# Top-32 attention and mixture of depths on one core: each stage of a unit in a step of its own

## The chip, the core and the metric

The kernel runs on one core of one Trainium2 chip. The core has TensorE (PE in the profile, with PEld for its weight loads), VectorE (DVE), ScalarE (ACT), GpSimd (POOL) and SyncE (SP, which here only issues DMAs); each works through its own queue in order. The metric is the device time of one execution in microseconds (us), the median of the runs shown. A lower time is better.

## The reference

The input has 8 batches, 8 heads, 576 tokens and 64 numbers per head and token. For every query the 32 largest of its 576 scores are kept, the rest is masked out, and the softmax of what is left weighs the values. The heads of a token are then put side by side (512 numbers), and in each batch the 128 tokens with the largest gate score pass through a two-layer network; its result, times a sigmoid of the gate, is added to them.

```python
scores = scale * np.matmul(q, k.transpose(0, 1, 3, 2))
kth = np.partition(scores, -top_k, axis=-1)[..., -top_k:-top_k + 1]
scores = np.where(scores >= kth, scores, -1000000000.0)
attn = np.exp(scores - np.max(scores, axis=-1, keepdims=True))
attn = attn / (np.sum(attn, axis=-1, keepdims=True) + 1e-09)
x = np.matmul(attn, v)                       # then (B, S, H*D)
scores = np.einsum('bsd,d->bs', x, w_gate)
top_idx = np.argpartition(-scores[b], capacity)[:capacity]
h = np.maximum(x[b, top_idx] @ w1, 0.0)
out[b, top_idx] = x[b, top_idx] + g[:, None] * (h @ w2)
```

All of it is computed in 32-bit floats. A second version of the whole computation stands behind a branch at the end (`general`); it runs only if a check on the device says that the fast way was not safe, and it does not run on these inputs.

## The kernel before, in words

**Units.** A unit is a batch, a query tile t and a pair of heads (line 513): 8 x 5 x 4 = 160 units. The 576 queries are cut into four tiles of 128 and a last one of 64 (`J = 4`, `JP = 512`, `R = 64`). A unit with t below 4 has two tiles of 128 queries, one per head (a whole unit); for t = 4 the 64 queries of both heads lie one above the other in one tile (a half unit, `heads_of`, line 219). Keys are split in the same way, 4 x 128 and 64.

**What a unit goes through.** (1) `multiply` (227): scores on PE into a PSUM tile `ps`; `keep` (242): ACT copies them to `sc`. (2) `bound` (252): DVE takes the 8 largest of each of 8 pieces (`cand`) and merges these 64 candidates in three rounds (`best`), which gives a lower bound for the 32nd score; POOL puts it into `seen` (the cast at line 270). (3) `part` (275): ACT forms the sign of score minus bound (`sides`); `mask` (290): POOL multiplies scores by it and adds 8 counters (`y`). (4) `find_kth` (302): DVE's maximum of `y` (`next8`), POOL scales it into `seen` (307). (5) Lines 544 to 556: ACT forms a steep ramp below the 32nd score (`z`, Relu), POOL subtracts it from the scores (`z`), so that what is masked out lies very low. (6) `turn` (309): PE transposes `z`, four blocks of 128 keys into `ptr` and the last 64 keys into `small`; ACT takes the exponential of both into `pT` (581, 589). (7) `values` (317): PE multiplies `pT` with the values `v`, for each head four blocks of 128 keys and one of 64, into `small`; ACT copies the result to `xs` (331).

**The loop.** One loop over n (line 530) runs all stages of different units side by side. Step n issues, in this order: loading of later inputs in the first steps (533), `multiply` of unit n+1 (536), the ramp and subtraction of unit n-2 (544), `keep` of n+1 (557), `values` of n-3 (559), `bound` of n (567), then tile by tile `part` and `mask` of n beside `turn` and exponential of n-2 (574), `find_kth` of n-1 (596), the gate of a finished token tile (600), one piece of the mixture (607), `normalise` (608) and a piece of loading the next batch (614). So `bound`, `part` and `mask` of one unit stand in one step, and so do the ramp, the transposes and the exponentials of another. `InOrder` (33) keeps PE, DVE, ACT and POOL in exactly the order in which the program issues; all instructions that pass through it have line 41 in the profile. DMAs are issued by SP in program order.

**The mixture.** `mixture` (388) is a generator that a batch's end starts; each step of the next batch takes one piece of it: the gate row (`route`, 348), ranks of the tokens (two DVE passes per tile with the table `before`, 370 to 386), one-hot picks, the gathered tokens (`xe_ps`, 40 PE instructions), two parts of the first layer (`h_ps`, 32 each), the second layer (`y_ps`, 16 of 512 columns) and an indirect DMA that adds the result to the output (481).

**Buffers.** PSUM: `ps` two tiles of two banks, `ptr` two banks, and two banks that `small`, the transposes of the loads (`tr`) and all of the mixture share (lines 84 to 86). SBUF: `sc` four buffers, `z`, `y`, `sides`, `cand`, `pT` two each.

Of the kernel before, what the change touches and what calls it, by code (L numbers as in the profile page):

```python
# [44 lines left out]
def kernel(  # L45
# [38 lines left out]
    ps_sc = ctx.enter_context(tc.tile_pool(name="ps_sc", bufs=2, space=PS))  # L84
    ps_tr = ctx.enter_context(tc.tile_pool(name="ps_tr", bufs=2, space=PS))
    ps_small = ctx.enter_context(tc.tile_pool(name="ps_small", bufs=2, space=PS))
# [28 lines left out]


    before = const.tile([P, NT, S], BF16, name="before")
    nc.gpsimd.memset(before[:, 0:J, JP:S], 0.0)
    nc.gpsimd.memset(before[:, 0:J, 0:JP], 1.0)
    nc.gpsimd.memset(before[:, J, :], 1.0)  # L120
    for t in range(J):
        nc.gpsimd.affine_select(
            out=before[:, t, 0:JP].rearrange("p (j i) -> p j i", j=J),
            in_=before[:, t, 0:JP].rearrange("p (j i) -> p j i", j=J),
            compare_op=ALU.is_gt,
            fill=0.0,
            base=t,
            pattern=[[-1, J], [-J, P]],
            channel_multiplier=J,
        )  # L130
    nc.gpsimd.affine_select(
        out=before[:, J, JP:S],
        in_=before[:, J, JP:S],
        compare_op=ALU.is_gt,
        fill=0.0,
        base=0,
        pattern=[[-1, R]],
        channel_multiplier=1,
    )
# [3 lines left out]
    for i in range(2):  # L143
        vt = const.tile([P, H, NT, DE], FP32, name=f"v{i}")
        nc.gpsimd.memset(vt, 1.0)
        vbufs.append(vt)
# [17 lines left out]
    def room_for_qkv(b):  # L164

        qT = kqpool.tile([P, NHP, S], FP32, name="qT")
        kT = kqpool.tile([P, NHP, S], FP32, name="kT")
        return qT, kT, vbufs[b % 2]

    def load_qkv(qb, kb, vb, qT, kT, vt):  # L170


        def fetch(src, hp, name):
            rows = ldpool.tile([P, NT, 2, D], FP32, name=name, tag="rows")
            for hh in range(2):
                nc.sync.dma_start(
                    out=rows[:, 0:J, hh, :],
                    in_=src[2 * hp + hh, 0:JP, :].rearrange("(p j) d -> p j d", j=J),
                )
            nc.sync.dma_start(  # L180
                out=rows[0:R, J, :, :],
                in_=src[2 * hp : 2 * hp + 2, JP:S, :].rearrange("h p d -> p h d"),
            )
            return rows

        todo = [
            (src, dst, hp, name)
            for hp in range(NHP)
            for src, dst, name in ((kb, kT, "kin"), (qb, qT, "qin"))
        ]  # L190
        fetched = {}
        for i, (src, dst, hp, name) in enumerate(todo):
            for j in range(i, min(i + 3, len(todo))):
                if j not in fetched:
                    fetched[j] = fetch(todo[j][0], todo[j][2], todo[j][3])
            rows = fetched[i]
            tr = ps_small.tile([P, 512], FP32, name="tr", tag="small")
            for c in range(J):
                pe.transpose(
                    tr[:, c * P : (c + 1) * P],  # L200
                    rows[:, c, :, :].rearrange("p h d -> p (h d)"),
                    ident,
                )
            act.copy(out=dst[:, hp, 0:JP], in_=tr)
            tr = ps_small.tile([P, 512], FP32, name="tr", tag="small")
            pe.transpose(
                tr[:, 0:R],
                rows[0:R, J, :, :].rearrange("p h d -> p (h d)"),
                ident[0:R, 0:R],
            )  # L210
            act.copy(out=dst[:, hp, JP:S], in_=tr[:, 0:R])
            nc.sync.dma_start(
                out=vt[:, i, 0:J, 0:D],
                in_=vb[i, 0:JP, :].rearrange("(p j) d -> p j d", j=J),
            )
            nc.sync.dma_start(out=vt[0:R, i, J, 0:D], in_=vb[i, JP:S, :])
            yield
# [9 lines left out]
    def multiply(t, hp, qT, kT):  # L227

        n = R if t == J else P
        pss = [ps_sc.tile([P, 2, 512], FP32, name="ps") for _ in heads_of(t)]  # L230
        for half in range(2):
            for ps, heads in zip(pss, heads_of(t)):
                for hh, r in heads:
                    d = slice(hh * D, (hh + 1) * D)
                    pe.matmul(
                        ps[r : r + n, half, 0:HALF],
                        qT[d, hp, t * P : t * P + n],
                        kT[d, hp, half * HALF : (half + 1) * HALF],
                    )
        return pss  # L240

    def keep(pss):

        sc = scpool.tile([P, 2, S], FP32, name="sc")
        for i, ps in enumerate(pss):
            act.copy(
                out=sc[:, i, :].rearrange("p (u s) -> p u s", u=2),
                in_=ps[:, :, 0:HALF],
            )
        return sc  # L250

    def bound(n, sc, at):

# [7 lines left out]
        for i in range(n):  # L261
            for u in range(8):
                dve.max(cand[:, i, 8 * u : 8 * u + 8], sc[:, i, u * w : (u + 1) * w])
            for r in range(3):
                dve.max(best[r][:, i, :], cand[:, i, :])
                if r < 2:
                    dve.match_replace(
                        cand[:, i, :], best[r][:, i, :], cand[:, i, :], LOWEST
                    )
        pool.tensor_copy(  # L270
            out=seen[:, 0, at : at + n],
            in_=best[2].rearrange("p i e -> p (i e)").bitcast(BF16)[:, 15 : 16 * n : 16],
# [29 lines left out]
    def find_kth(n, y, at):  # L302

        next8 = stats.tile([P, 2, 8], FP32, name="next8")
        for i in range(n):
            dve.max(next8[:, i, :], y[:, i, :])
        pool.tensor_scalar_mul(seen[:, 1, at : at + n], next8[:, 0:n, 7], BIG)

    def turn(i, z, tr, small):

        for c in range(J):
            pe.transpose(
                tr[:, c * P : (c + 1) * P], z[:, i, c * P : (c + 1) * P], ident
            )
        pe.transpose(small[0:R, i * P : (i + 1) * P], z[:, i, JP:S], ident)

    def values(t, hp, pT, small, vt, xs):

        n = R if t == J else P
        for i, heads in enumerate(heads_of(t)):  # L320
            for hh, r in heads:
                for c in range(NT):
                    rows = R if c == J else P
                    pe.matmul(
                        small[0:n, 2 * P + hh * DE : 2 * P + (hh + 1) * DE],
                        pT[0:rows, c, i, r : r + n],
                        vt[0:rows, 2 * hp + hh, c, :],
                        start=(c == 0),
                        stop=(c == J),
                    )  # L330
        act.copy(
            out=xs[0:n, 2 * hp : 2 * hp + 2, :].rearrange("p h e -> p (h e)"),
            in_=small[0:n, 2 * P : 2 * P + 2 * DE],
# [14 lines left out]
    def route(gate, rank):  # L348

        gate_row = modpool.tile([P, S], FP32, name="gate_row")  # L350
        tr = ps_small.tile([P, 512], FP32, name="tr", tag="small")
# [7 lines left out]
        tr = ps_small.tile([P, 512], FP32, name="tr", tag="small")  # L359
# [5 lines left out]
        for t in range(NT):  # L365
            if t == 3:
                yield
            n = R if t == J else P
            tied = modpool.tile([P, S], FP32, name="tied", tag="scratch")
            dve.scalar_tensor_tensor(  # L370
                out=tied[0:n, :],
                in0=gate_row[0:n, :],
                scalar=gate[0:n, t : t + 1],
                in1=before[0:n, t, :],
                op0=ALU.is_equal,
                op1=ALU.mult,
            )
            dve.scalar_tensor_tensor(
                out=tied[0:n, :],
                in0=gate_row[0:n, :],  # L380
                scalar=gate[0:n, t : t + 1],
                in1=tied[0:n, :],
# [3 lines left out]
            )  # L386

    def mixture(row0, x, gate):
# [4 lines left out]
        rank = modpool.tile([P, NT], FP32, name="rank")  # L393
        yield from route(gate, rank)
# [30 lines left out]
        ps = ps_small.tile([P, 512], FP32, name="xe_ps", tag="small")  # L425
# [14 lines left out]
        ps = ps_small.tile([P, 512], FP32, name="extra_ps", tag="small")  # L440
# [10 lines left out]
        dve.tensor_copy(out=row_i, in_=ps[:, 0:1])  # L451
# [4 lines left out]
        for f0 in range(0, NFC, 4):  # L456
            yield
            ps = ps_small.tile([P, 512], FP32, name="h_ps", tag="small")
# [14 lines left out]
        ps = ps_small.tile([P, 512], FP32, name="y_ps", tag="small")  # L473
# [41 lines left out]
    load_from = per_batch - 1 - 2 * NHP  # L515
# [5 lines left out]
    loading = load_qkv(q[0], k[0], v[0], *qkv[0])  # L521
    mixing = iter(())
    gating = None
    xs = x = gate = None
    scs, masked, turned = {}, {}, {}

    def tiles_of(n):
        return len(heads_of(units[n][1]))

    for n in range(-1, len(units) + 4):  # L530
        is_unit = lambda i: 0 <= i < len(units)

# [3 lines left out]
        pss = None  # L536
        if is_unit(n + 1):
            b, t, hp = units[n + 1]
            pss = multiply(t, hp, *qkv[b][0:2])
# [4 lines left out]
        if is_unit(n - 2):  # L544
# [12 lines left out]
        if pss is not None:  # L557
            scs[n + 1] = keep(pss)
        if is_unit(n - 3):
            b, t, hp = units[n - 3]  # L560
# [5 lines left out]
            values(t, hp, *turned.pop(n - 3), qkv[b][2], xs)  # L566
        if is_unit(n):
# [192 lines left out]
```

## Time and profile before

| What | Before |
|---|---|
| Median of 3 runs (lowest to highest) | 1587.45 us (1572.88 to 1592.38) |
| The profiled execution, its own time | 1579.77 us |
| Its span, first to last instruction | 1578.0 us |
| Mean granted PE clock, as a share of full speed | 0.756 |
| Busy: PE, DVE, POOL, ACT | 1345.1, 1077.1, 1003.9, 887.5 us |
| First score copies of batches 1 to 7 | 185.4, 376.7, 568.0, 759.3, 950.7, 1141.2, 1332.5 us |
| Last exponential of the last unit; end | 1526.4; 1578.0 us |

How to read it: a row of the timeline gives the start, the time until the last of its instructions ended, the engine, the operation, what it writes and reads, and how many instructions were merged; in brackets the idle time of the engine before it and what ended it. PE and PEld rows of one matmul belong together: PEld loads the stationary side, PE moves the other through the array. A 32-bit matmul stands as two instructions, a transpose as one. "PEclk" is the share of its full clock that PE was granted.

From one score copy of a whole unit to the next the steps of the later batches take 8.4 to 14.3 us, and the pattern repeats from batch to batch, every 191.3 us or so.

### The profile page before, as it was taken

To read this page: it belongs to the slowest core of one execution; us is meant where nothing else is said; L and a number is where in the kernel's file an instruction comes from. 1 tells how busy PE (TensorE), PEld (TensorE's weight loads), DVE (VectorE), ACT (ScalarE), POOL (GpSimd) and SP (SyncE) were. 2 spreads that over 40 slices of the span, in tenths; PEclk is the share of its full clock that TensorE was granted. 3 is DMA by queue.
4 is the path that set the end of the run, shared out by engine and by line. 5 is a ranking of instruction groups with operands and counts; after the bars stand their busy time and mean duration, and the time that the engine had idled before them with its cause. 6 is when DMAs were issued, how large, how long until landed. Compare 5 with 4: busy or idle time off the path is not lost.

```text
span 1578.0 us, 24253 instructions
## 1 busy us (share of the span) xinstructions
PE 1345.1 (85%) x7322; PEld 1047.6 (66%) x7322; DVE 1077.1 (68%) x5024; ACT 887.5 (56%) x1953; POOL 1003.9 (64%) x1253
## 2 busy tenths in 40 slices
PE   5988888888889879988789887998888988889866
PEld 3766667676677657767568665786666766677554
DVE  4786598656986469764797549875499654987631
ACT  3666565655555555555655556565565665555630
POOL 4776676665766657665666657666576665766730
PEclk9677867967679685786868768597766977679767
DMA  7301200012001120011200112001120011000000
GB/s 177 80 1 31 72 19 1 16 31 73 11 2 22 31 72 5 1 23 31 73 4 1 30 31 69 1 1 31 46 53 1 1 37 35 4 1 7 1 31 9
DMA packets 120507, 45.95 MB, mean 29 GB/s; under 512 B 116144, under 2 KB 116144, under 8 KB 119344
## 3 DMA queue, kind: packets, MB, share of 16 engines
q1 hardware_dynamic: 119216, 42.23, 10.8%
q0 software_dynamic: 1152, 2.10, 1.0%
q8 instruction: 60, 0.98, 0.3%
q14 instruction: 79, 0.65, 0.1%
HBM read 32.77 MB, written 11.53 MB: 28 GB/s over the span
## 4 chain that ended last, share of the span: by engine, by line
PE 42%; DVE 29%; POOL 12%; ACT 10%; issue 6%; DMA 0%; SPq 0%; POOLq 0%; ACTq 0%
PE small L41 18%; DVE cand L41 13%; PE ps L41 7%; POOL z L41 6%; PE ptr L41 6%; DVE best L41 5%; DVE tied L41 5%; ACT sides L41 4%; PE h_ps L41 3%; PE xe_ps L41 3%; DVE next L41 3%; PE y_ps L41 3%; ACT pT L41 3%; PE tr L41 3%; POOL y L41 2%
## 5 line engine op out<-in xcount | busy, mean ns | idle before, releaser
L41 PEld LDWEIGHTS small<-v,pT 128*128 128x128 f32 (+3 forms) x3200 | 492.3, 230 | 150.2 <-ACT pT L41 55.0
L41 PE MATMUL small<-v,pT 128*128 128x65 f32 (+3 forms) x3200 | 560.0, 329 | 16.3 <-ACT pT L41 15.7
L41 POOL TENSOR_TENSOR y<-sc,sides 128x576 f32<-128x576 f32 x288 | 375.3, 1303 | 271.1 <-ACT sides L41 242.0
L41 POOL TENSOR_TENSOR z<-sc,z 128x576 f32<-128x576 f32 x288 | 410.7, 1446 | 153.3 <-ACT z L41 152.3
L41 DVE MAX8 cand<-sc 128x8 f32<-128x72 f32 x2304 | 333.6, 217 | 124.5 <-ACT sc L41 124.5
L41 PE MATMUL ptr<-ident,z 128*128 128x128 f32 x1152 | 251.2, 358 | 101.7 <-POOL z L41 100.9
L41 ACT ACTIVATE z<-sc,seen 128x576 f32<-128x576 f32 x288 | 208.9, 768 | 153.0 <-POOL seen L41 152.9
L41 DVE MAX8 next<-y 128x8 f32<-128x584 f32 x288 | 210.2, 755 | 104.6 <-POOL y L41 104.2
L41 ACT ACTIVATE sides<-sc,seen 128x576 bf16<-128x576 f32 x288 | 222.0, 771 | 104.7 <-POOL seen L41 104.3
L41 PE MATMUL ps<-kT,qT 64*128 64x288 f32 (+1 forms) x1280 | 273.4, 549 | 1.5 <-ACT qT L41 1.5
L41 PEld LDWEIGHTS ptr<-ident,z 128*128 128x128 f32 x1152 | 171.2, 180 | 143.8 <-POOL z L41 133.6
L41 DVE MAX8 best<-cand 128x8 f32<-128x64 f32 x864 | 197.0, 228 | 29.8
L41 PEld LDWEIGHTS ps<-kT,qT 64*128 64x128 f32 (+1 forms) x1280 | 144.8, 230 | 53.1 <-issue 19.9
L41 ACT COPY sc<-ps 128x576 f32<-128x576 f32 x288 | 168.7, 630 | 13.2 <-PE ps L41 7.1
L41 ACT ACTIVATE pT<-ptr 128x512 f32<-128x512 f32 x288 | 167.8, 583 | 9.4 <-PE ptr L41 9.0
L41 ACT COPY xs<-small 128x130 f32<-128x130 f32 (+1 forms) x160 | 43.0, 268 | 207.1 <-PE small L41 207.1
L41 DVE MATCH_REPLACE8 cand<-best,cand 128x64 f32<-128x64 f32 x576 | 120.2, 209 | 0.0
L41 DVE TENSOR_SCALAR sums<-xs 128x8 f32<-128x8 f32 (+1 forms) x40 | 13.8, 344 | 135.4 <-ACT xs L41 135.4
L41 PE MATMUL small<-ident,z 128*64 128x128 f32 x288 | 100.8, 350 | 0.0
L41 POOL TENSOR_SCALAR y<-steps,seen 128x8 f32<-128x8 f32 x288 | 86.0, 299 | 22.6
L41 PE MATMUL tr<-ident,kin 128*128 128x128 f32 (+1 forms) x160 | 36.9, 344 | 42.3 <-ACT kT L41 32.9
L41 PE MATMUL tr<-ident,qin 128*128 128x128 f32 (+1 forms) x160 | 37.5, 349 | 41.1 <-ACT qT L41 29.2
(69 smaller groups left out, 1050.1 us busy)
## 6 DMA issues: line engine op xcount, KB each, us to landing
kin<-in_k_dram SPq DMA_DIRECT2D x64, 128.0 KB, 2.9
qin<-in_q_dram SPq DMA_DIRECT2D x64, 128.0 KB, 2.9
v<-in_v_dram SPq DMA_DIRECT2D x64, 128.0 KB, 2.6
out_dram<-x SPq DMA_DIRECT2D x8, 1024.0 KB, 4.6
w<-in_moe_w_dram SPq DMA_DIRECT2D x2, 2048.0 KB, 10.1
kin<-in_k_dram SPq DMA_DIRECT2D x32, 32.0 KB, 2.5
qin<-in_q_dram SPq DMA_DIRECT2D x32, 32.0 KB, 2.5
v<-in_v_dram SPq DMA_DIRECT2D x64, 16.0 KB, 2.3
```

The source lines that it names most:

```text
L41: return lambda *a, **kw: self._tc.keep_in_program_order(fn(*a, **kw))
```

## The change

**A step for each stage.** Step n of the new loop holds: transposes of unit n-3, values of n-4, scores of n+1 on PE; `find_bound` of n and `find_kth` of n-1 on DVE; `part` and `mask` of n-1, exponentials of n-3, ramp of n-2, `keep` of n+1 and the copy of the values of n-4 on ACT; mask of n-1, subtraction of n-2, and at the end of the step both small `seen` writes (`cut` of n, `lift` of n-1) on POOL. A unit's `part` therefore comes one step after its bound, its transposes one step after its ramp, and its values one step after its exponentials, as before.

**PE's order in a step** for whole units: transposes of tile 0 (4), values of tile 0 (8 instructions), transposes of tile 1 (4) and of the last keys (1), scores against keys 0 to 511 (4 instructions of 512 columns), values of tile 1 (8) and of the last keys of both heads (2 of 130 columns), scores against keys 512 to 575 (4 of 64 columns).

**Last keys of both heads together.** For whole units the last 64 keys of the two heads lie beside each other in `z`, are transposed by one instruction into a corner of `ps` and multiplied with `vpair`, whose two halves of partitions hold the values of the two heads with zeros beside them. `ps` is now one tile of four banks with one buffer, `av` (values) has one bank with one buffer, and loads and mixture share one bank, `misc`.

**Merges of two tiles alternate** in `find_bound`. **Ranks in one pass:** the second DVE pass and the table `before` are gone; ranks of all batches are added up at the end, and equal gates would send the kernel to `general`. **Loads:** the last keys and queries of all heads come in one DMA each and are transposed together (8 instructions) in a piece of their own, so that loading of a batch begins one step earlier. The last check stands after the last mixture.

```diff
-    ps_sc = ctx.enter_context(tc.tile_pool(name="ps_sc", bufs=2, space=PS))
+    ps_sc = ctx.enter_context(tc.tile_pool(name="ps_sc", bufs=1, space=PS))
     ps_tr = ctx.enter_context(tc.tile_pool(name="ps_tr", bufs=2, space=PS))
-    ps_small = ctx.enter_context(tc.tile_pool(name="ps_small", bufs=2, space=PS))
+    ps_av = ctx.enter_context(tc.tile_pool(name="ps_av", bufs=1, space=PS))
+    ps_misc = ctx.enter_context(tc.tile_pool(name="ps_misc", bufs=1, space=PS))
...
-            for r in range(3):
+        for r in range(3):
+            for i in range(n):
                 dve.max(best[r][:, i, :], cand[:, i, :])
-                if r < 2:
+            if r < 2:
+                for i in range(n):
                     dve.match_replace(
                         cand[:, i, :], best[r][:, i, :], cand[:, i, :], LOWEST
                     )
...
+    def turn_last(n, z, ps):
+        last = z.rearrange("p i s -> p (i s)")[:, JP : JP + n * R]
+        tr = ps[0 : n * R, 1024 - P : 1024]
+        pe.transpose(tr, last, ident)
+        return tr
...
+        if i == 1:
+            pe.matmul(
+                av[:, 0 : 2 * DE],
+                last,
+                vpair[:, hp, :, :].rearrange("p h e -> p (h e)"),
+                start=False,
+                stop=True,
+                skip_group_check=True,
+            )
...
+            dve.tensor_scalar(
+                out=junk[0:n, :],
                 in0=gate_row[0:n, :],
-                scalar=gate[0:n, t : t + 1],
-                in1=tied[0:n, :],
+                scalar1=gate[0:n, t : t + 1],
+                scalar2=None,
                 op0=ALU.is_gt,
                 op1=ALU.add,
                 accum_out=rank[0:n, t : t + 1],
             )
...
+        if tiles_of(n - 3) or tiles_of(n + 1):
+            ps = ps_sc.tile([P, 4 * 512], FP32, name="ps")
+        for i in range(2):
+            if i < tiles_of(n - 3):
+                trs.append(turn(i, z))
+                if i == tiles_of(n - 3) - 1:
+                    trs.append(turn_last(i + 1, z, ps))
+            if i == 1 and tiles_of(n + 1):
+                b, t, hp = units[n + 1]
+                multiply(t, hp, qkv[b][0], ps, slice(0, JP))
+            if i < tiles_of(n - 4):
+                values(t4, hp4, i, *weights[n - 4], av, qkv[b4][1])
+        if tiles_of(n + 1):
+            multiply(t, hp, qkv[b][0], ps, slice(JP, S))
+        if tiles_of(n):
+            bests[n] = find_bound(tiles_of(n), scs[n])
+        if tiles_of(n - 1):
...
+                part(i, scs[n - 1], first_tile[n - 1], sides)
+                mask(i, scs[n - 1], first_tile[n - 1], sides, y)
+            next8 = find_kth(tiles_of(n - 1), y)
+        if tiles_of(n - 3):
...
+                act.activation(
+                    pT[:, i, :, :],
+                    trs[i].rearrange("p (c i) -> p c i", c=J),
+                    AF.Exp,
+                    scale=scale,
+                )
+            act.activation(last[0 : w * R, :], trs[w], AF.Exp, scale=scale)
...
+        if tiles_of(n + 1):
+            scs[n + 1] = keep(tiles_of(n + 1), ps)
+        if tiles_of(n - 4):
...
+            keep_values(t, hp, av, xs)
...
+        if tiles_of(n):
+            cut(tiles_of(n), bests.pop(n), first_tile[n])
+        if tiles_of(n - 1):
+            lift(tiles_of(n - 1), next8, first_tile[n - 1])
```

## Prediction

> **What bounds the kernel now.** I read the page first: PE is the busiest engine, at a clock that changes throughout.
>
> ```profile
> span 1578.0 us, 24253 instructions
> PE 1345.1 (85%) x7322; PEld 1047.6 (66%) x7322; DVE 1077.1 (68%) x5024; ACT 887.5 (56%) x1953; POOL 1003.9 (64%) x1253
> ...
> PEclk9677867967679685786868768597766977679767
> ```
>
> Next the stretches of 3.413 us, inside which the granted clock never changed (each change in this trace lies on that grid), for two ordinary steps:
>
> ```profile
> 330.77:334.18 3.41, 3.41 (x15) 2.94 (x15) 0.00 (x0) 0.00 (x0) 0.69 (x2) 0.50 0.00 0
> 334.18:337.59 3.41, 3.17 (x14) 2.70 (x14) 2.87 (x20) 3.33 (x9) 2.11 (x3) 0.50 0.02 5
> 337.59:341.01 3.42, 2.98 (x21) 2.14 (x22) 3.25 (x16) 2.56 (x5) 3.18 (x5) 1.00 0.27 62
> 341.01:344.42 3.41, 3.01 (x24) 2.46 (x23) 3.24 (x18) 1.26 (x4) 2.43 (x4) 1.00 0.11 24
> 344.42:347.83 3.41, 1.12 (x10) 0.61 (x9) 0.96 (x3) 2.55 (x7) 3.09 (x5) 1.00 0.00 0
> 347.83:351.25 3.42, 3.42 (x16) 2.65 (x12) 1.86 (x9) 1.96 (x3) 2.53 (x3) 0.50 0.38 86
> ```
>
> The clock (third last column) is 1.00 or 0.50, and busy time does not decide it: 330.77 is wholly busy and stays at half. Columns moved do. In full-clock time a transpose or a 128-column matmul instruction moves for 0.107 us, a pair of 288-column score instructions for 0.242, a values instruction of 65 columns for 0.054, though with 128-wide weights the next starts only 0.112 later. Window 334.18 is all transposes (13, up to 1.4 us) and the next is full; 330.77 holds 12 values instructions and a transpose (0.75), and 344.42 eight score instructions (1.0), and after each comes half. Counted so over the trace's 448 windows, all that led to full clock held at least 1.29 us, all that led to half at most 1.39. I take 1.34.
>
> Last the timeline of these steps, for prices at full clock (339 to 343) and at half (348 to 360):
>
> ```profile
> 339.35 2.87 PE L41 MATMUL small<-v,pT 128*128 128x65 f32 x20
> ...
> 342.15 0.66 PE L41 MATMUL ptr<-ident,z 128*128 128x128 f32 x4
> ...
> 348.05 1.44 ACT L41 ACTIVATE z<-sc,seen 128x576 f32<-128x576 f32 x2 [0.71 <-POOL seen L41]
> ...
> 348.36 5.10 PE L41 MATMUL small<-v,pT 128*128 128x65 f32 x20
> ...
> 348.90 2.77 POOL L41 TENSOR_TENSOR z<-sc,z 128x576 f32<-128x576 f32 x2 [0.89 <-ACT z L41]
> ...
> 353.39 1.11 PE L41 MATMUL ptr<-ident,z 128*128 128x128 f32 x4
> ...
> 356.10 0.36 ACT L41 ACTIVATE pT<-small 64x256 f32<-64x256 f32 x1
> ...
> 357.61 2.18 PE L41 MATMUL ps<-kT,qT 64*64 64x288 f32 x8
> ```
>
> At half clock PE alone fills a step: 5.0 + 2.3 + 2.1 = 9.4 us, more with a load's transposes. At full clock another chain ends last: `seen` 0.2, ramp 0.85, subtractions 2.8, bound 0.2, sign 1.0, masks 3.0, the last maximum 0.7, or 8.4 with the handovers overlapped. Steps take 8.4 (full clock) to 11.4; ordinary whole steps of a later batch average 9.84.
>
> **The change, part by part.**
>
> *The new chain.* In the changed program's order, with its waits, the exponential of the last keys waits for the step's last score matmul: both lie in `ps`, and it stands on ACT ahead of both ramps, both score copies and the `xs` copy. POOL's first subtraction waits for the first ramp, and the next step's first transpose, which stands first on PE, for that subtraction. So nothing of PE's run overlaps: step = PE's whole run + gap. In the old order a step's transposes used the `z` of the same step, and scores and values could run meanwhile.
>
> *PE's run.* At full clock: 9 transposes x 0.109 = 0.98; 16 values instructions x 0.112 = 1.79; 2 of 130 columns, 0.22; scores of 512 columns, 2 pairs x 0.242 x 512/288 = 0.86; those of 64 columns, bound by weight loads, 0.215; three changes of tile size at 0.14 (what the 64-row values instructions add in single rows), with 0.1 for two exposed loads: 4.58 us. At half: 1.92 + 3.41 + 0.43 + 1.71 + 0.43 + 0.58 + 0.11 = 8.60. The old run by the same prices: about 5.1 and 9.5. Joining the last keys thus saves some 0.5 us of PE at full clock, most of it tile changes. A switch between transposing and multiplying in one tile size shows nowhere: between 0 and 0.14, and I take 0.05.
>
> *The gap.* Matmul tail 0.16 to 0.21; handover 0.04; last exponential until the ramp can start 0.17; ramp 0.77; handover 0.09; subtraction 1.40; handover 0.05: 2.70 us. The step is 7.3 us at full clock, 11.35 at half.
>
> *Which clock.* A run moves columns for 9 x 0.107 + 16 x 0.054 + 0.86 + 0.22 + 0.11 = 3.0 us. At 7.3 us a step, a window that begins more than 2.4 us into the run catches less than 1.34, the gap being nearly empty; two windows are 6.83 us, so every step has such a window, and the clock falls. At half clock the densest stretch is second transposes, 512-column scores, start of the second values: a window that begins 1.6 to 3.1 us into the run moves 1.34 to 1.47, so the next is full. That next window shortens the rest of the run and is then mostly gap (0.6 moved), so half returns. The step settles where it lasts three windows, 3 x 3.413 = 10.24 us: 1.11 us below the half-clock step, reached when the full window begins 6.38 us into the run, so the one ahead of it at 2.97, inside 1.6 to 3.1. A longer step moves the windows earlier in the run, so more of it is at full clock: it corrects itself.
>
> *Batch.* 11 whole steps without mixture matmuls x 10.24 = 113. Four with half units in transposes and values: runs of 3.5 (full) to 6.1, steps 6.2 to 8.9; the window containing their long values stretch is often full afterwards, so 8.0, together 32. Five mixture steps: `xe_ps` 4.4, `h_ps` 3.5 twice, `y_ps` 6.9 us at full clock, which they earn; what exceeds the gap is added, and with one `misc` bank the load's transposes wait for the eviction (0.6) and add 0.5 to 0.9 ahead of the next run: with `xe_ps` 7.5 (run, partly at half) + 4.4 + 0.85 + 1.1 = 13.9; then 8 without much PE work; `h_ps` 4.6 + 3.6 + 0.85 + 0.5 = 9.6 at full clock, and the first of them 11.8 to 15.1, 13.5, because the clock has fallen in the light step; `y_ps` 4.6 + 7.1 + 0.9 + 0.5 = 13.1: 58. Sum 203 against 191.3. Seven batches: 7 x 11.7 = +82. The first batch, 174.7 long without mixture, becomes four filling steps (35) and 16 x 10.24: +24. Tail: one more short step (+4), one rank pass less (5 x 0.82, -4). Span 1578 + 106 = 1684, own time 1686. The profiled execution ran 7.7 us below the median of the runs (1579.8 against 1587.45); I say 1690.
>
> *Edits at nothing.* Alternating merges: a maximum followed by an independent instruction lets it start after 0.15, by a dependent one after 0.25, so about 0.85 us a whole step; DVE then works some 5.6 us in 10.24 and hides it; uncovered it is worth 128 x 0.85 = 109 us at most. Rank passes: five times the first pass gone, 0.82 alone to 1.87 beside POOL, also under DVE's idle time; the remaining pass is bounded by the 0.70 maximum of 584 and that 1.87. Both small `seen` writes at the end of POOL's step: bound, sign 0.98, masks 3.1, subtractions 2.8, 0.2 = 7.1 us, under 10.24; at full clock a second bound as tight as the first. Single `ps` and `av` buffers make the last-key transpose and the values wait for ACT's copies, which end 2.9 us after the last matmul, when PE is still in its first transposes. SP: 29 load DMAs a batch in place of 40, issued well ahead; at the start the two new ones cost at most two issues, 1.3 us. POOL's first fills stay beside the first loads.
>
> A rule against this change: the Trainium skill, "TensorE: Matmul & The Clock Gate", section "Part 4: PE-mode transpose", says that transposes do not count as busy for the clock. Window 334.18 speaks against it: transposes alone, and full clock next. By the page, 2.0 us a step would count, no window would reach 1.34, all steps would be at half, and the time would be some 1850.
>
> **Rivals.** *Faster:* PE's run gets at least the clock 0.756 that the old kernel has on average; then it lasts 6.05, a step 8.75, a batch 11 x 8.75 + 27 + 55 = 178, the whole about 1490; wholly at full clock, 155 a batch and 1270. For it: the run is 0.5 us shorter and its densest parts stand together. Against: three windows attract. It decides above 0.64 in the run (4.58 / (9.84 - 2.70)); the settled step has 0.61, so little is needed. *Half throughout:* the threshold lies above 1.47 for this mix; ordinary steps 11.35, batch 225, about 1850. Against: rises at 1.29 to 1.35. *No change:* ordinary steps near 9.8 because runs vary with load transposes; 1556 to 1619. That the chain isn't there is excluded by the waits.
>
> **How the numbers follow.** Forecast (three windows) 0.51, 1620 to 1760; half throughout 0.08; no measurable change 0.15; faster 0.26, of which 0.19 around 1490 (1430 to 1555) and 0.07 below. The range leaves out the 0.08 above and the 0.07 below: 1450 to 1760; the forecast alone has 1625 to 1750. Faster by over 2% (about what a measurement can tell from no change) 0.26, within 0.15, slower 0.59.
>
> **What would show it.** Right: the first transpose of every whole step waits for POOL `z`, PE idle about 2.3 to 2.7 us there; steps of 10.2 us, one window in three at full clock; mean clock 0.65 to 0.75; DVE idle rising. Wrong: PE gaps under 1.5 us, ordinary steps below 9, or full clock through several ordinary steps.

## The result, and the profile after

| What | Before | After |
|---|---|---|
| Median of 4 runs each (lowest to highest) | 1582.89 us (1572.88 to 1592.38) | 1643.22 us (1640.47 to 1644.45) |
| Ratio after / before, 95% interval | | 1.038 (1.031 to 1.045) |
| Profiled execution: own time, span, mean clock | 1579.77, 1578.0 us, 0.756 | 1643.82, 1641.9 us, 0.739 |
| A later batch, first score copy to first score copy | 191.3 us | 198.0 us |

The change made the kernel slower by 3.8%. In the runs below the kernel before took from 1532 us at a mean clock of 0.792 to 1593 us, while the changed one stayed within 4 us; so the experiments are compared with 1643.2 us by their medians.

The page of the changed kernel: PE has 384 instructions less and is busy for 51.9 us less, and DVE is busy for 192.6 us less, but the whole takes longer.

```profile
span 1641.9 us, 23197 instructions
...
PE 1293.2 (79%) x6938; PEld 941.0 (57%) x6938; DVE 884.5 (54%) x4986; ACT 861.0 (52%) x1897; POOL 969.5 (59%) x1254
```

The waits of the changed kernel (waiting engine and tile, what it waited for, us in total, times, longest):

```profile
ACT last L41 <- PE ps L41: 414.6, 148, 6.3
POOL z L41 <- ACT z L41: 374.2, 149, 6.4
...
PE ptr L41 <- POOL z L41: 293.5, 132, 4.3
```

These three are the links of the forecast's chain, in its order: the exponential of the last keys waits for the scores, the subtraction for the ramp, the transposes for the subtraction. In the kernel before the first did not exist, and the last two were shorter:

```profile
POOL z L41 <- ACT z L41: 152.3, 120, 3.4
...
PE ptr L41 <- POOL z L41: 100.9, 106, 2.0
```

The timeline of one ordinary step of the changed kernel:

```profile
282.39 1.11 PE L41 MATMUL ptr<-ident,z 128*128 128x128 f32 x4 [2.52 <-POOL z L41]
...
288.11 1.26 PE L41 MATMUL av<-v,pT 128*128 128x65 f32 x8
...
289.58 0.44 PE L41 MATMUL ps<-kqT 64*128 64x64 f32 x4
...
290.06 0.28 ACT L41 ACTIVATE last<-ps 128x128 f32<-128x128 f32 x1 [3.47 <-PE ps L41]
290.24 1.43 ACT L41 ACTIVATE z<-sc,seen 128x576 f32<-128x576 f32 x2
...
291.09 2.77 POOL L41 TENSOR_TENSOR z<-sc,z 128x576 f32<-128x576 f32 x2 [2.93 <-ACT z L41]
...
292.54 1.12 PE L41 MATMUL ptr<-ident,z 128*128 128x128 f32 x4 [2.53 <-POOL z L41]
```

The last score matmul ends at 290.02, the exponential starts at 290.06, the ramp at 290.24, the subtraction at 291.09, and its first half releases the next transposes at 292.54. PE was idle for 2.53 us, and the step from transposes to transposes took 10.15 us. The clock (third last column) in the windows of that step:

```profile
281.64:285.05 3.41, 2.66 (x13) 2.66 (x14) 2.97 (x24) 2.29 (x6) 2.65 (x5) 0.50 0.02 5
285.05:288.47 3.42, 3.42 (x12) 1.58 (x10) 1.89 (x10) 1.53 (x4) 2.87 (x4) 0.50 0.00 0
288.47:291.88 3.41, 1.55 (x14) 1.29 (x13) 2.31 (x7) 1.82 (x4) 0.79 (x1) 1.00 0.00 0
```

One window in three is full, and it is the one in which PE is idle more than half the time. Counted as in the forecast, in full-clock time, the three windows move columns for 0.9, 1.4 and 0.7 us: the one ahead of the full window, with the scores, earned the clock, and the gap uses it up.

### The profile page after: what moved, and what is told of

The parts are those of the page before. It is cut to its first block, busy times and chain, and to the rows that moved or that the text cites. A ratio compares the mean times of both kernels' runs of the same rounds, so it can differ in the third digit from the quotient of the medians.

```text
span 1641.9 us, 23197 instructions
## 1 busy us (share of the span) xinstructions
PE 1293.2 (79%) x6938; PEld 941.0 (57%) x6938; DVE 884.5 (54%) x4986; ACT 861.0 (52%) x1897; POOL 969.5 (59%) x1254
## 4 chain that ended last, share of the span: by engine, by line
PE 73%; POOL 14%; ACT 9%; issue 3%; DMA 1%; DVE 1%; ACTq 0%; SPq 0%; POOLq 0%
PE av L41 27%; PE ps L41 21%; PE ptr L41 14%; POOL z L41 12%; ACT z L41 6%; PE h_ps L41 4%; PE y_ps L41 3%; PE xe_ps L41 3%; POOL y L41 1%; PE tr L41 1%; POOL out_dram L540 1%; ACT sides L41 1%; ACT hT L41 1%; DMA rows<-in_q_dram 0%; ACT pT L41 0%
## 5 line engine op out<-in xcount | busy, mean ns | idle before, releaser
L41 POOL TENSOR_TENSOR z<-sc,z 128x576 f32<-128x576 f32 x288 | 405.6, 1426 | 375.2 <-ACT z L41 374.2
L41 PEld LDWEIGHTS av<-v,pT 128*128 128x128 f32 (+1 forms) x2560 | 403.6, 247 | 180.0 <-issue 170.1
L41 PE MATMUL av<-v,pT 128*128 128x65 f32 (+1 forms) x2560 | 434.5, 332 | 0.4 <-ACT xs L41 0.4
L41 PE MATMUL ps<-kqT 64*128 64x64 f32 (+3 forms) x1280 | 350.2, 645 | 2.7 <-ACT kqT L41 2.7
L41 ACT ACTIVATE last<-ps 128x128 f32<-128x128 f32 (+1 forms) x160 | 44.1, 276 | 437.8 <-PE ps L41 414.6
L41 PEld LDWEIGHTS ps<-kqT 64*128 64x128 f32 (+1 forms) x1280 | 122.9, 230 | 89.4 <-issue 68.4
L41 DVE MAX8 best<-cand 128x8 f32<-128x64 f32 x864 | 154.6, 216 | 3.3
L41 PE MATMUL tr<-ident,rows 128*128 128x128 f32 x256 | 46.4, 309 | 25.5 <-ACT hT L41 8.2
L41 PE MATMUL h_ps<-xeT,w 128*128 128x128 f32 x512 | 61.4, 278 | 1.1 <-ACT hT L41 0.7
L41 PE MATMUL av<-vpair,last 128*128 128x130 f32 x256 | 61.3, 324 | 0.0
L41 ACT COPY kqT<-tr 128x512 f32<-128x512 f32 x72 | 43.0, 598 | 33.6 <-PE tr L41 33.6
## 6 DMA issues: line engine op xcount, KB each, us to landing
w<-in_moe_w_dram SPq DMA_DIRECT2D x2, 2048.0 KB, 11.7
```

The lines of the kernel that those rows point to most:

```text
L41: return lambda *a, **kw: self._tc.keep_in_program_order(fn(*a, **kw))
```

## The experiments

Theory: PE's run and the vector work stand one after the other in every step, because the exponential of the last keys waits for the last score matmul and stands ahead of the ramps; the gap that this leaves then holds the clock down. Rivals: the wait is shown but something else binds; the clock follows something other than moved columns; the lost cover of DVE's work; a plain chain without any lock (a lock here means that a step settles at three clock windows, 10.24 us, although its chain gets somewhat longer). The clock and the profile lines of a run are those of its one profiled execution (in e1 the one of 1394.5 us, in e10 that of 1341 us), the times are medians.

**e1: the exponential behind the ramps.**

```diff
-            act.activation(last[0 : w * R, :], trs[w], AF.Exp, scale=scale)
-            weights[n - 3] = pT, last
...
                 pool.tensor_tensor(z[:, i, :], sc[:, i, :], z[:, i, :], ALU.subtract)
             zs[n - 2] = z
+        if tiles_of(n - 3):
+            act.activation(last[0 : w * R, :], trs[w], AF.Exp, scale=scale)
+            weights[n - 3] = pT, last
```

> Edit on the changed kernel: ScalarE issues the exponential of the last keys behind both ramps of the step instead of ahead of them. Theory (the ramp, the first subtraction and the next step's first transpose wait, through that exponential, for the last score matmul): with the exponential behind, the ramp can start as soon as the kept mask is there, and TensorE's run and the vector chain overlap again. The step is then bounded by GpSimd's own 7.1 us or by the run, 4.6 us at full and 8.6 us at half clock, whichever is longer: 7.1 to 8.8 us in place of 10.24, some 11 to 14 steps of a batch of 20 gain 1.4 to 3 us each, and the whole falls from 1643 to 1350 to 1520 us. Rival (the wait is shown but something else ends just behind it, for instance the last-key transpose or the values waiting for single buffers): within 2% of 1643 us.

Measured: 1413.95 us (1394.5 to 1424.82), 0.895 of the kernel before (0.887 to 0.903); mean clock 0.818. Waits:

```profile
ACT last L41 <- PE ps L41: 178.4, 109, 3.4
...
PE ptr L41 <- POOL z L41: 123.2, 84, 4.3
...
DVE cand L41 <- ACT sc L41: 112.7, 68, 8.6
```

Moving one instruction of 0.28 us a step gives 229 us. POOL's subtraction now waits 5.7 us in all for the ramp, in place of 374.2. The theory's chain was there and was what cost; the rival is out. The rival named the single buffers too: already in the changed kernel PE's instructions into `av` wait 0.4 us in all for ACT's copies. The exponential still waits 178 us for the scores, now with the score copies behind it, and DVE waits for those.

**e6: the last scores ahead of the second values.** The chain opened from its other end, on PE.

```diff
                 multiply(t, hp, qkv[b][0], ps, slice(0, JP))
+                multiply(t, hp, qkv[b][0], ps, slice(JP, S))
             if i < tiles_of(n - 4):
                 values(t4, hp4, i, *weights[n - 4], av, qkv[b4][1])
-        if tiles_of(n + 1):
-            multiply(t, hp, qkv[b][0], ps, slice(JP, S))
```

> Edit on the changed kernel: TensorE does the scores against keys 512 to 575 directly behind those against keys 0 to 511, ahead of the second tile's values in place of behind them; the exponential of the last keys keeps its place ahead of the ramps. Theory (the exponential waits for the last score matmul, which shares its PSUM tile, not for TensorE's run as such): the second values (1.4 us at full clock, 2.6 at half, with the last keys) leave the chain and fill the gap; steps fall to 7.1 us (GpSimd's own work) to 8.8 us, the whole to 1350 to 1500 us. Rival (ramp and transposes wait for the end of TensorE's step, whatever stands there): within 2% of 1643 us.

Measured: 1413.22 us (1411.52 to 1421.96), 0.907 (0.898 to 0.916); clock 0.795. So it is the last score matmul that ACT waits for, not the end of PE's step. The exponential reads the transposed last keys, which PE has finished 3.8 us earlier in the step shown above (286.18 and 290.02), but they lie in the same PSUM bank as the scores of head 0 against keys 512 to 575 (columns 896 to 1023 and 512 to 575 of `ps`, banks of 512 columns).

**e7: both.** The diffs of e1 and e6 together.

> Both edits together on the changed kernel: exponential of the last keys behind the ramps, and the scores against keys 512 to 575 ahead of the second tile's values. Theory: each edit alone already takes TensorE's tail out of the chain, so both together bring little over the better of them, 1360 to 1430 us. Rival (each takes away a part of the chain of its own): 60 us or more below 1414 us.

Measured: 1333.91 us (1330.9 to 1337.3), 0.854 (0.846 to 0.863), clock 0.839. My theory fell here: the second edit brought another 80 us. The waits say why:

```profile
PE ptr L41 <- POOL z L41: 170.4, 106, 4.4
...
ACT last L41 <- PE ps L41: 43.8, 43, 2.6
...
DVE cand L41 <- ACT sc L41: 36.0, 25, 7.8
```

What e1 had left, the late exponential in front of the score copies, was a wait of its own: with the scores earlier it falls from 178.4 to 43.8 us and DVE's wait for the copies from 112.7 to 36.0.

**e3: work in the gap.** The chain stays; PE transposes the identity into a tile that nobody reads, so this run holds extra work.

```diff
             multiply(t, hp, qkv[b][0], ps, slice(JP, S))
+            if n < per_batch or not 10 <= n % per_batch < 15:
+                fill = ps_misc.tile([P, 512], FP32, name="fill", tag="misc")
+                for c in range(16):
+                    pe.transpose(fill[:, (c % 4) * P : (c % 4 + 1) * P], ident, ident)
```

> Edit on the changed kernel: sixteen more transposes of the identity into a block that nobody reads, behind the last scores of every step but those that carry mixture matmuls; they are extra work, 16 x 0.107 us = 1.7 us of moved columns at full clock, in what was TensorE's gap of 2.5 to 2.7 us. Theory (the clock of a window is set by the columns that moved in the one before, and the gap is what loses it): every window now moves over 1.34 us, the clock stays at 1.0 in ordinary steps, the run lasts 4.6 us and the step 7.3 to 7.6 us; the whole falls to 1280 to 1400 us although TensorE does more. Rival (the clock is not decided so, for instance because transposes do not count): the clock stays near 0.67, sixteen transposes at half clock take 3.5 us of which 0.8 to 1 us overhang the gap, and the whole is 1640 to 1800 us.

Measured: 1423.95 us (1418.25 to 1439.27), 0.902 (0.896 to 0.909); clock 0.937. The theory's mechanism holds; its figure was at least 24 us too low, in part because steps without filling lose the clock (in batch 1 two mixture steps of 15.1 us at 0.84 and 10.1 at 0.66, which take 12.1 and 9.0 in the changed kernel). Score copies of ordinary steps in it:

```profile
225.31 1.17 ACT L41 COPY sc<-ps 128x576 f32<-128x576 f32 x2
...
232.72 1.17 ACT L41 COPY sc<-ps 128x576 f32<-128x576 f32 x2
...
240.14 1.17 ACT L41 COPY sc<-ps 128x576 f32<-128x576 f32 x2
```

They are 7.41 us apart at full clock (forecast: 7.3); the other ordinary steps of that batch take 6.9 to 8.7. So 2000 more PE instructions, and 219 us less. All that was added are transposes, so transposes hold the clock up. The Trainium skill, "TensorE: Matmul & The Clock Gate", section "Part 4: PE-mode transpose", has it that they do not count as busy for the clock; the 32-bit transposes of this run contradict it, 0.937 against 0.739.

**e2 and e5: a longer gap.** Three copies on ACT between the exponential and the ramp, and then one.

```diff
+    spare = const.tile([P, P], FP32, name="spare")
...
             weights[n - 3] = pT, last
+            for _ in range(3):
+                act.copy(out=spare, in_=ident)
```

> Edit on the changed kernel: three more ScalarE copies of a 128x128 block into a block that nobody reads, between the exponential of the last keys and the first ramp, so 0.5 to 0.8 us more in the chain of every step. Theory (steps settle at three clock windows, 10.24 us, because a longer step moves more of the run to full clock): ordinary steps stay at 10.1 to 10.3 us at a mean clock that rises to 0.70 to 0.73, and the whole grows by less than 1.5% (under 25 us). Rival (a plain chain, run plus gap, at whatever clock): 160 steps x 0.5 to 0.8 us = 80 to 130 us more, 5 to 8%, ordinary steps 10.7 to 11.0 us.

Measured: 1794.39 us (1791.99 to 1797.13), 0.94 us a step or 9.2% more; clock 0.697. The lock that I had forecast did not hold. The rival's plain chain was right in kind, but its 5 to 8% were exceeded too. The three copies stand as one row, with 0.86 us from its start to the ramp's, and steps wholly at half clock appear:

```profile
483.19 0.28 ACT L41 ACTIVATE last<-ps 128x128 f32<-128x128 f32 x1 [4.70 <-PE ps L41]
483.36 0.95 ACT L41 COPY spare<-ident 128x128 f32<-128x128 f32 x3
484.22 1.44 ACT L41 ACTIVATE z<-sc,seen 128x576 f32<-128x576 f32 x2
485.56 1.15 ACT L41 COPY sc<-ps 128x576 f32<-128x576 f32 x2
```

The copy before this one stood at 473.32, 12.24 us earlier: the forecast's 11.35 of a half-clock step plus 0.86. Such steps stand among others of mostly 10.4 to 11 us. One copy (`range(1)`) asks whether there is a lock with an edge, or none.

> Edit on the changed kernel: one more ScalarE copy (0.295 us in the run with three) between the exponential of the last keys and the first ramp. The run with three showed no lock: the whole grew by 0.94 us a step. Theory now (the lock exists, but has an edge: it needs a window that begins 1.6 us or more into the half-clock run and is followed by a full one; the full one then saves at most (8.60 - 1.60 - 3.41) / 2 = 1.79 us, so run plus gap may be 10.24 + 1.79 = 12.03 us at most; three copies make 11.35 + 0.88 = 12.23, one copy 11.65): with one copy ordinary steps stay at 10.2 us and the whole within 1.5% of 1643 us. Rival (no lock, the 10.2 us were chance): 160 x 0.3 = 47 us more, 2.9%, ordinary steps 10.5 us.

Measured: 1681.76 us (1678.62 to 1683.91), 2.3% more, between both. But in this batch the ordinary steps stay where they were:

```profile
674.27 1.16 ACT L41 COPY sc<-ps 128x576 f32<-128x576 f32 x2
...
684.47 1.16 ACT L41 COPY sc<-ps 128x576 f32<-128x576 f32 x2
...
692.96 0.28 ACT L41 ACTIVATE last<-ps 128x128 f32<-128x128 f32 x1 [3.32 <-PE ps L41]
693.14 0.29 ACT L41 COPY spare<-ident 128x128 f32<-128x128 f32 x1
693.32 1.44 ACT L41 ACTIVATE z<-sc,seen 128x576 f32<-128x576 f32 x2
694.67 1.16 ACT L41 COPY sc<-ps 128x576 f32<-128x576 f32 x2
...
704.88 1.16 ACT L41 COPY sc<-ps 128x576 f32<-128x576 f32 x2
```

The score copies are 10.20, 10.20 and 10.21 us apart; in the changed kernel these steps take 10.1 to 10.2. The copy lengthened the chain by less than its own 0.29 us: from the exponential to the ramp it is 0.36 us here (692.96 to 693.32) and 0.17 in the changed kernel (290.06 to 290.24), so 0.19 more. With three copies it is 1.03, so 0.86 more. So the lock exists, and has an edge between 0.19 and 0.86 us more. The time went elsewhere. A batch of the changed kernel (198.0 us) and one of this run (204.7; two of its batches take as long, four 201.4 to 201.5) differ, by kinds of step, as follows: four with half units 35.6 to 38.3, five with mixture 53.4 to 56.7, the seven ordinary between them 67.5 to 71.3 (the changed kernel has one of 7.4 us at full clock and one of 9.0 at 0.81 there, where this batch has locked ones), the last four 41.5 to 38.3.

**e4: merges one after the other again.**

```diff
-        for r in range(3):
-            for i in range(n):
+            for r in range(3):
                 dve.max(best[r][:, i, :], cand[:, i, :])
-            if r < 2:
-                for i in range(n):
+                if r < 2:
                     dve.match_replace(
```

The merges of a tile now stand in the loop over the tiles, directly behind that tile's candidates.

> Edit on the changed kernel: the merges of two tiles stand one after the other again, as in the kernel before, in place of alternating. Theory (VectorE is idle for several us of every step, so what the alternation saves hides nowhere): VectorE's busy time rises by some 43 us and the time stays within 0.5% of 1643 us. Rival (the merges are on the path): 128 units x 0.85 us = up to 109 us more, 6.6%.

Measured: 1643.7 us (1639.6 to 1645.91): no difference. DVE's busy time rises from 884.5 to 997.0 us, by 112.5 and not by 43; I had taken only the maxima, and the forecast's 109 us was the right size. It is all hidden. Most of the rest of the 192.6 us by which DVE is less busy comes from the ranks, whose passes took 94.6 us before and take 32.2 now.

**e11: serial merges on both edits.** On the kernel of e7 the merges of the first tile, then those of the second, here behind the candidates of both.

> On the changed kernel with both edits: the merges of two tiles one after the other in place of alternating. Theory (in steps of 7.3 us VectorE's 5.6 + 0.85 us come close to the step, and the bound it finds is what GpSimd's small write and with it the next signs wait for): part of the 0.85 us now shows, 128 x 0.2 to 0.5 us, 25 to 65 us more than 1334. Rival (still hidden, as in the changed kernel, where it made no difference): within 1% of 1334 us.

Measured: 1346.96 us (1345.51 to 1348.4), 13 us or 1.0% above e7, in another group of runs. Less than I expected, and just within the rival's 1%: DVE's busy time rises by 85 us (913.3 to 998.6), of which some 13 show, even where most ordinary steps take about 7 to 8.3 us.

**e12: ranks made twice.** The pass that remains is repeated for every tile, its second result unread.

```diff
+            again = modpool.tile([P, 1], FP32, name="again")
+            dve.tensor_scalar(
+                out=junk[0:n, :],
+                in0=gate_row[0:n, :],
...
+                accum_out=again[0:n, :],
+            )
```

> Edit on the changed kernel: the remaining rank pass is made twice, its second result unread: 40 VectorE instructions of 0.8 us more, 32 us in all, about what the dropped passes cost. Theory (VectorE's idle time hides them): within 0.5% of 1643 us. Rival (the ranks of a batch lie on the path, gate row to picks to gathered tokens): up to 32 us more, 2%.

Measured: 1652.62 us (1649.81 to 1655.37), 9.4 us or 0.57% more, a little beyond the theory's 0.5%. The repetition adds 31.4 us of DVE time, about half of the 62 us by which the rank passes fell. Batches stay at 198.0 us and PE waits for the picks only once, in the tail, so in the batches it is hidden; of the spans' difference of 11.1 us, 9.7 arise after the last batch's first score copy. PE at the end of the changed kernel:

```profile
1606.36 8.99 PE L41 MATMUL xe_ps<-pick,x 128*128 128x128 f32 x40 [5.64 <-DVE pick L41]
1616.02 1.36 PE L41 MATMUL extra_ps<-extra,pick 128*128 128x2 f32 x10 [0.68 <-ACT xeT L41]
1617.79 3.81 PE L41 MATMUL h_ps<-xeT,w 128*128 128x128 f32 x32 [0.41 <-DVE g L41]
```

and of this run:

```profile
1612.14 10.95 PE L41 MATMUL xe_ps<-pick,x 128*128 128x128 f32 x40 [9.92 <-DVE pick L41]
1623.77 2.38 PE L41 MATMUL extra_ps<-extra,pick 128*128 128x2 f32 x10 [0.68 <-ACT xeT L41]
1626.56 6.13 PE L41 MATMUL h_ps<-xeT,w 128*128 128x128 f32 x32 [0.41 <-DVE g L41]
```

PE's wait for the picks grows by 9.92 - 5.64 = 4.28 us, five passes of 0.86; then the three groups take 1.96 + 1.02 + 2.32 = 5.30 us longer, because the clock stays at half for 27.3 us there in place of 10.2. A wait in the tail was paid twice over.

**e8, e9, e10: filling on the open chain.** Six transposes as in e3 on the kernel of e1 (e8); six and twelve at the end of PE's order on the kernel of e7, in the nine steps of a batch without half units and mixture (e9, e10). All three hold extra work that nobody reads; the edit of e9, to which that of e7 comes:

```diff
+        if 4 <= n % per_batch < 10 or 15 <= n % per_batch < 18:
+            fill = ps_misc.tile([P, 512], FP32, name="fill", tag="misc")
+            for c in range(6):
+                pe.transpose(fill[:, (c % 4) * P : (c % 4 + 1) * P], ident, ident)
```

> On the changed kernel with the exponential of the last keys behind the ramps (1414 us): six transposes of the identity into a block that nobody reads are added behind the last scores of every step but those with mixture matmuls, 0.65 us more of moved columns. Theory (in that kernel half of the ordinary steps, 9.5 to 9.7 us long, run at half clock because some window moves under 1.34 us; a step of 7.1 us then moves 3.0 + 0.64 us, 1.75 a window): most ordinary steps run at full clock and last 7.1 to 7.5 us, the whole 1280 to 1370 us. Rival (extra work on an engine that is busy 85% of the span only costs): 160 x 0.65 to 1.3 us, of which some hides: 1420 to 1520 us.

Measured: 1389.7 us (1373.25 to 1416.09), clock 0.873. Between both expectations. Two of its four runs (1373 and 1375 us) lie below all of e1's, the other two (1404 and 1416) among them: not settled. The clock rose, yet steps of 9.3 to 10.9 us at 0.5 to 0.7 remain.

> On the changed kernel with both edits (exponential of the last keys behind the ramps, scores against keys 512 to 575 ahead of the second tile's values; 1334 us, mean clock 0.839): six transposes of the identity into a block that nobody reads are added at the end of TensorE's order in nine steps of a batch of 20, those without half units and without mixture matmuls. Theory (those steps still move between full and half clock, 5 to 8 of the 9 below full; at full clock they last 7.2 us by GpSimd's own work): they settle at 7.2 to 7.4 us where they now take 7.0 to 8.3, so 0.3 to 0.8 us x 9 x 8 = 20 to 60 us less, 1275 to 1315 us. Rival (the clock no longer decides, GpSimd does): within 1% of 1334 us.

Measured: 1320.92 us (1317.48 to 1329.38), clock 0.876: 1.0% below e7, in another group of runs, so at best a small gain; the expected 1275 to 1315 was missed, and the rival's 1% just holds.

> As the run with six, with twelve transposes, 1.3 us of moved columns more in each of the nine steps. Theory: two windows then always hold their share, the nine steps are at full clock throughout at 7.2 to 7.4 us, 1270 to 1300 us, no worse than with six, since TensorE's 4.6 + 1.3 us stay below GpSimd's 7.1. Rival (extra work costs TensorE): worse than with six by up to 72 x 0.65 = 47 us.

Measured: 1333.89 us (1331.58 to 1341.03), clock 0.887: 13 us above e9, as the rival had it, and no gain over e7; the expected 1270 to 1300 was missed. The clock rose and the time did not follow, so with the chain open the clock is hardly the limit any more. The chain of work that ended last, in shares of the span, for the changed kernel and for e7:

```profile
PE 73%; POOL 14%; ACT 9%; issue 3%; DMA 1%; DVE 1%; ACTq 0%; SPq 0%; POOLq 0%
...
PE 40%; POOL 30%; ACT 14%; DVE 10%; issue 5%; DMA 1%; SPq 0%; POOLq 0%; ACTq 0%
```

The best versions are e7 and e9, 19% and 20% below the changed kernel (1333.9 and 1320.9 of 1643.2).

## Why the prediction was right

Right in sign and in the chain it named. The figure, 1690 us, was 47 us (2.8%) too high: of a forecast growth of 103 us 60 came. The lock that it took for every ordinary step holds for fewer than half of them in a later batch.

- *The new chain.* Right, link by link. e1 and e6 open it at either end, for 229 and 230 us. Why ACT waits: the Trainium skill, "PSUM — Partial Sum Buffer", section "PSUM bank collisions raise a hardware error", says that the compiler back end orders any two instructions of different engines on one bank and quadrant of partitions. That would give the wait of 414.6 us its cause, but the trace shows less: the exponential starts 0.05 us after the last of the step's score matmuls, which writes head 1's scores in the next bank, and 0.16 after head 0's (medians). So what is shown is a wait for the last score matmul into the tile `ps`; no run here separates the bank from the tile, since the transposed keys were not tried in a bank of their own.
- *The run and the gap.* Right. 7.41 us at full clock (e3) for a forecast 7.3, 12.24 less 0.86, so 11.38, at half clock (e2) for 11.35 (its own terms, 8.60 + 2.70, make 11.30); PE idle for 2.5 us.
- *Which clock.* Right that the moved columns set it, transposes among them (e3). Counted in the same way over the traces of all fourteen kernels, every window that led to full clock held at least 1.2 us of moved columns, and every one that led to half at most some 1.5; in the changed kernel 1.29 and 1.35. That ordinary steps settle near 10.24 us holds in part. Of the eleven of a later batch five take 10.1 to 10.5 us at 0.66 to 0.67; the others take 7.4 us at full clock, 9.0 at 0.81, and four from 9.6 to 11.2 at 0.57 to 0.64. A step below 9 was a sign of being wrong, and there is one a batch. In the first batch, without mixture, twelve steps in a row take 10.0 to 10.2. "It corrects itself" was too general. The forecast's own working has an edge: the window ahead of the full one must begin 1.6 us or more into the run, so the full one saves at most (8.60 - 1.60 - 3.41) / 2 = 1.79 us, and half-clock run plus gap may reach 12.03. Changed kernel: 11.30; with one copy 11.49, still locked; with three 12.16, no longer. I didn't work that out before e2.
- *The batch.* 203 forecast, 198.0 measured, with errors that in part cancel. The terms: ordinary steps 113, measured 109.0 (the mean, 9.9, comes from steps of 7.4 to 11.2); half-unit steps 32, measured 35.6; mixture steps 58, measured 53.4. The largest single miss is the first `h_ps` step, 13.5 forecast and 9.7 measured: the clock fell for one window in the light step ahead of it (520.57 to 523.99) and was full again 2 us before `h_ps` began. First batch: +24 forecast, measured 196.2 - 174.7 = +21.5. Of the 42 us by which the span was overestimated, the six batches from the second on are 33 (70 forecast, 1184.4 - 1147.1 = 37 measured), the last batch with the tail 8.5 (11.7 forecast, 3.2 measured) and the first 2.5; the first score copy stood 1.9 us later, which was not forecast.
- *Edits at nothing.* Alternating merges: right, 112 us of DVE time and no difference (e4), where the forecast said 109 at most. Rank passes: hidden in the batches, not in the tail (e12); the forecast had 4 us for the tail, and repeating the pass cost 9.7 there, because the clock followed.
- *The rivals.* Half throughout is out (a mean of 0.739). Faster was the right second case: the clock was what was missing, and e3, which holds it up with extra work, shows steps of 7.4 us. The 0.64 itself was not tested.

The gain that the change could bring is there, and the placing of one small exponential hid it: with that and the last scores moved, the same design takes 0.854 of the time before.

## What to carry to other kernels

When stages are spread over steps, follow the smallest instruction too: one of 0.28 us that reads a PSUM tile which is still being written, and stands ahead of the next stage's first instruction, puts two engines one after the other. Price such a gap twice where the clock depends on work done: as idle time, and as the slower clock of what follows. A quick test for the second is useless work in the gap; if the kernel gets faster, the gap was costing the clock.

## What the runs showed of the hardware

- Work that nobody reads made the kernel faster: 2000 transposes, 1643 to 1424 us, clock 0.739 to 0.937 (e3).
- Steps lock to three clock windows, 10.2 us, over a range of at least 0.19 us of the gap (changed kernel, e5), and leave it before 0.86 (e2). Whole batches lock too: the later ones of the changed kernel take 197.93 to 197.99 us, and 58 windows of 3.4133 us are 197.97; in e5 they take 201.4 or 204.8, 59 or 60 windows.
- The threshold of 1.34 us of moved columns is met almost exactly by 128-column matmuls issued back to back at half clock: `xe_ps` in e12's tail took 10.95 us for 40, so 12.5 a window of 3.413, 12.5 x 0.107 = 1.33 us, and the clock stayed at half; in the changed kernel's tail the same matmuls, started at half clock, had full clock after two windows.
- Two alternating chains on DVE overlap: 112 us less busy time over 128 whole units, while a single maximum of a merge went only from 228 to 216 ns (e4 and the changed kernel).
